# Eight FFN rounds behind an attention stage: low parts on VectorE, longer route leads, conversions split around the token chunks

## The chip, the cores and the metric

The kernel runs on one core of one Trainium2 chip. The metric is the device time of one execution in microseconds (us), as the median of runs; lower is better. Engines are named as in the profile: PE is the matmul engine (PEld its weight load), DVE is VectorE, ACT is ScalarE, POOL is GpSimd, SP issues most of the DMAs.

## The reference

Three stages in float32. First an mLSTM-like attention over 4 batches, 8 heads, 768 steps and head size 40 gives x with 3072 rows of 320. Then a mixture of experts, in which each token goes to one of 8 experts of 384 places, handed out in falling order of all logits:

```python
logits = x @ w_gate
for idx in np.argsort(-logits.flatten()):
    tok, e = idx // 8, idx % 8
    if assigned[tok] >= 0 or counts[e] >= 384: continue
    assigned[tok] = e; counts[e] += 1
for e in range(8):
    mask = assigned == e
    y[mask] = np.maximum(x[mask] @ w1[e], 0.0) @ w2[e]   # 320 -> 1024 -> 320
```

Last a gated layer that is the same for all tokens: `out = ((y @ w_a) * (y @ w_b)) @ w_out`, 320 to 1536 to 320.

## The kernel before, in words

The attention stage (up to about 200 us) is not touched. Behind it come eight **rounds**, one for each expert in the order in which experts fill up (`ffn`, L1000). A round takes its 384 tokens through both layers:

- *g phase*: `g1(f)` (L1040, 8 matmuls each, f = 0 to 7) makes a 128x384 piece of the hidden layer from the token tiles xh, xl and the expert's weights w1h, w1l; `g2(f)` (L1051, 8 matmuls each) adds it into three sums called acc with w2.
- *handover* (L1082 to L1090): the three sums become yh and yl.
- *ab phase*: `ab(f)` (L1095, 16 matmuls, f = 0 to 11) makes a and b, and `outp(f)` (L1113, 9 matmuls of 320 columns) adds the product into the output sums. `tail` (L1136) writes a round's output rows, within the next round.

Every float32 factor is split into a **high part** (an ACT copy to float32r) and a **low part** (the value minus the high part), so each product needs up to three matmuls. Low parts of the hidden pieces are tiles `ml`: in the g phase DVE makes them (L1048) right behind the ACT high part, in the ab phase POOL does (L1110), once for each f. The next expert's weights are loaded raw and converted by `split_w` (L907), eight pieces a round: for w1 ACT makes w1h (L914), POOL the low part w1l (L918), DVE the low part of the last 64 rows (L919); for w2 ACT makes the high part (L926), POOL two low parts (L927 of 2x64, L929 of 2x256 columns).

Which tokens come next is found by `route(r)` (L667), a chain that runs beside the matmuls of the round before: DVE compares keys with 128 thresholds (three tiles `G` for one count, L660), PE counts with 24 small matmuls (`rt`, L684), DVE tests the count (`okb`, L703), PE sums that over the rows (L706), DVE makes new thresholds (`d`, L712), five times over; then an L752 step, and `place` (L789), which ends in the token list `idx` and PE's L817. `keys` (L618) begins the next route at once. Only DVE and PE work on it, and each is in order, so a late `G` stops PE in the middle of the round's matmuls.

The order is written out while the program is built: `mm` (L981) counts 0.155 for each matmul, and the generators (route, next weights, late conversions) go on when the count reaches what they last yielded. The numbers after `yield` thus say how many matmuls PE gets between two steps; they are leads, not waits. Route yields are multiplied by 1.25 from route 2 on. The next weights (`weights`, L845) start at the handover: load, wait for idx, gather the tokens by an indirect DMA on POOL (`xg`, L857), convert all eight pieces, then transpose the tokens (`prep_x`, L945, PE L955):

```python
        yield 1.0
        if r:
            yield from sw
...
        yield from self.prep_x(r, xg)
        yield from sw
```

In round 0 five late conversions of the shared layer's weights (`conv`, L115, with `rawb == 1`) run as well: DVE L121, L124, L127, ACT L133 and L135 (or L154), POOL L136 and L138 (or L155).

Of the kernel before, what the change touches and what calls it, by code (L numbers as in the profile page):

```python
# [43 lines left out]
class Kern:  # L44
# [70 lines left out]
    def conv(self, pool, kind, i, raw, more, nxt):  # L115
# [11 lines left out]
        V.tensor_tensor(F, F, sg, op=OP.mult)  # L127
# [539 lines left out]
    def route(self, r):  # L667
# [10 lines left out]
        def count(Gs, d, nthr):  # L678
# [14 lines left out]
            if r:  # L693
                yield 1.0
                for j in range(3):
                    mms(j)
# [3 lines left out]
        def total(cnt, on):  # L700
# [3 lines left out]
            yield 0.8  # L704
# [84 lines left out]
    def place(self, r, wm):  # L789
# [36 lines left out]
        if r:  # L826
            yield 1.0
            for j in range(3):
                mms(j)
# [15 lines left out]
    def weights(self, r):  # L845
# [4 lines left out]
        if r == 0:  # L850
            for _ in range(2):
                next(sw)
        while r not in self.idx:
# [7 lines left out]
        if r:  # L861
            yield from sw
# [44 lines left out]
    def split_w(self, r):  # L907
# [3 lines left out]
        def one(j):  # L911
# [5 lines left out]
            e = V if r == 0 and j < 2 else P  # L917
            e.tensor_sub(l, raw[:, 0:2], h[:, 0:2].bitcast(F32))  # L918
# [4 lines left out]
        def two(i):  # L923
# [76 lines left out]
    def ffn(self):  # L1000
# [34 lines left out]
        for r in range(E):  # L1035
# [3 lines left out]

            def g1(f):  # L1040
# [7 lines left out]
                V.scalar_tensor_tensor(hl, p, 0.0, hh.bitcast(F32), op0=OP.max, op1=OP.subtract)  # L1048
                hq[f] = (hh, hl)

            def g2(f):  # L1051
# [3 lines left out]
                mm(yp[2], w[:, 256:384], hh, start=st, stop=False)  # L1055
                mm(yp[2], w[:, 256:384], hl, start=False, stop=sp)
                for m in range(2):
                    wh = w[:, m * 128:m * 128 + 128]
# [29 lines left out]
            for c in range(2):  # L1088
                self.split_act(yh, yl, c, yp[c])
# [5 lines left out]
            def ab(f):  # L1095
# [3 lines left out]
                for k in range(2):  # L1099
# [9 lines left out]
                e = V if r + 1 == E and f == NF2 - 1 else nc.gpsimd  # L1109
                e.tensor_sub(gl, gf, gh.bitcast(F32))  # L1110
# [118 lines left out]
```

## Time and profile before

| | us |
|---|---|
| median of 3 runs | 910.32 (910.04 to 911.11) |
| the profiled execution | 908.78 |
| its span, first to last instruction | 907.1 |
| PE busy in the span | 820.5 (90%) |
| DVE busy | 537.7 (59%) |
| POOL busy | 415.8 (46%) |
| ACT busy | 353.8 (39%) |
| mean granted clock | 0.957 of full |

The profiled execution is 1.7 us longer than its span and 1.5 us shorter than the median. Times below are us from the start of the span. The granted clock is PE's share of its full 2.4 GHz; it has two levels here, 1.0 and 0.5. Matmuls overlap, so their recorded lengths (some 340 ns) are about twice the step from one to the next.

### The profile page before, as it was taken

What the parts mean: (1) busy time and instruction counts of PE and PEld (TensorE: products, weight loads), DVE (VectorE), ACT (ScalarE), POOL (GpSimd) and SP (SyncE); (2) the same over time, 40 slices, a digit from 0 to 9 for tenths busy, and PEclk for the clock granted to TensorE, in tenths of its full rate; (3) what the DMA queues carried; (4) which work ended last, traced back from release to release, by engine and by line L of the source; (5) the groups of instructions that cost most, each with busy time, mean ns of one, the idle gap of its engine ahead of it and who ended that gap; (6) DMA issues with size and microseconds to landing.
All of it is one profiled execution on the core that took longest, in us unless ns stands there. A gap on an engine that the chain in (4) does not pass through costs nothing.

```text
span 907.1 us, 15899 instructions
## 1 busy us (share of the span) xinstructions
PE 820.5 (90%) x5939; PEld 777.9 (86%) x5939; DVE 537.7 (59%) x1188; ACT 353.8 (39%) x721; POOL 415.8 (46%) x440
## 2 busy tenths in 40 slices
PE   5779889885888899979989999999999999999996
PEld 3678778774777889979879998999899999999996
DVE  6777888856866885676576587476764212311211
ACT  4877678610443332232233234224322532532321
POOL 4576777731423670464056338233723823532122
PEclk9998999995898989989989999999999999999999
DMA  6875777523222310220120122031111301200000
GB/s 180 256 222 168 232 231 216 151 69 85 66 66 83 93 51 16 75 76 19 57 74 24 35 81 59 1 96 48 30 53 45 106 24 44 76 1 23 1 1 22
DMA packets 51038, 73.84 MB, mean 81 GB/s; under 512 B 6161, under 2 KB 41361, under 8 KB 50961
## 3 DMA queue, kind: packets, MB, share of 16 engines
q1 hardware_dynamic: 41744, 45.30, 17.5%
q10 hardware_dynamic: 6912, 19.66, 6.6%
q0 software_dynamic: 2304, 7.87, 2.7%
q8 instruction: 47, 0.77, 0.4%
q14 instruction: 31, 0.25, 0.1%
HBM read 63.37 MB, written 7.86 MB: 79 GB/s over the span
## 4 chain that ended last, share of the span: by engine, by line
PE 66%; DVE 14%; ACT 10%; issue 4%; DMA 3%; POOL 1%; ACTq 1%; DVEq 0%; POOLq 0%; SPq 0%
PE ring L982 33%; PE acc L982 20%; DVE G L660 3%; PE pq L400 2%; PE rt L684 2%; PE pv L431 2%; DVE w1h L919 1%; ACT mq L194 1%; PE pe L392 1%; DVE gf L1105 1%; PE pl L490 1%; PE pg L416 1%; ACT dd L394 1%; DMA mraw<-in_wab_dram 1%; ACT yh L978 1%
## 5 line engine op out<-in xcount | busy, mean ns | idle before, releaser
L1110 POOL TENSOR_TENSOR ml<-gf,mh 128x384 fp32r<-128x384 f32 x95 | 106.6, 1122 | 266.4 <-ACT mh L1107 265.9
L982 PE MATMUL ring<-yh,wh 128*128 128x384 f32 x576 | 202.2, 351 | 6.4 <-ACT yh L978 4.6
L982 PE MATMUL ring<-yl,wh 128*128 128x384 f32 x576 | 136.8, 344 | 0.0
L982 PE MATMUL ring<-yh,wl 128*128 128x384 f32 x384 | 132.6, 345 | 0.0
L1105 DVE TENSOR_TENSOR gf<-ring,at 128x384 f32<-128x384 f32 x96 | 53.3, 555 | 127.2 <-PE ring L982 123.3
L1107 ACT ACTIVATE mh<-gf 128x384 fp32r<-128x384 f32 x96 | 50.4, 525 | 187.4 <-DVE gf L1105 187.4
L982 PEld LDWEIGHTS ring<-yh,wh 128*128 128x128 f32 x576 | 111.4, 193 | 13.8 <-ACT yh L978 7.2
L660 DVE TENSOR_TENSOR G<-thc,d 128x1024 bf16<-128x1024 int16 (+1 forms) x90 | 110.4, 1245 | 0.4
L982 PEld LDWEIGHTS ring<-yl,wh 128*128 128x128 f32 x576 | 105.6, 193 | 0.1
L982 PE MATMUL acc<-woh,ml 128*128 128x320 f32 x288 | 91.7, 318 | 0.0
L982 PE MATMUL acc<-woh,mh 128*128 128x320 f32 x288 | 90.7, 315 | 0.0
L982 PE MATMUL acc<-wol,mh 128*128 128x320 f32 x288 | 90.5, 314 | 0.0
L982 PE MATMUL acc<-mh,w 128*128 128x384 f32 x320 | 88.9, 341 | 0.0
L1046 ACT ACTIVATE mh<-ring 128x384 fp32r<-128x384 f32 x64 | 31.5, 492 | 133.3 <-PE ring L982 127.9
L1048 DVE SCALAR_TENSOR_TENSOR ml<-ring,mh 128x384 fp32r<-128x384 f32 x64 | 35.5, 556 | 79.4 <-ACT mh L1046 76.8
L1103 ACT ACTIVATE at<-ring 128x384 f32<-128x384 f32 x96 | 46.8, 487 | 79.9 <-PE ring L982 76.7
L982 PEld LDWEIGHTS ring<-yh,wl 128*128 128x128 f32 x384 | 74.3, 194 | 0.0
L918 POOL TENSOR_TENSOR w1l<-raw,w1h 128x512 fp32r<-128x512 f32 x30 | 43.9, 1468 | 51.2 <-ACT w1h L914 51.1
L982 PE MATMUL ring<-xh,w1h 128*128 128x384 f32 x192 | 65.9, 343 | 0.1
L982 PE MATMUL acc<-ml,w 128*128 128x384 f32 x192 | 65.2, 339 | 0.5 <-DVE ml L1048 0.5
L982 PEld LDWEIGHTS acc<-mh,w 128*128 128x128 f32 x320 | 58.6, 190 | 0.3 <-issue 0.3
L982 PEld LDWEIGHTS acc<-woh,ml 128*128 128x128 f32 x288 | 55.3, 192 | 2.5 <-POOL w L929 2.2
(212 smaller groups left out, 1721.6 us busy)
## 6 DMA issues: line engine op xcount, KB each, us to landing
raw<-in_moe_w_dram SPq DMA_DIRECT2D x32, 320.0 KB
raw<-in_moe_w_dram SPq DMA_DIRECT2D x32, 256.0 KB
vk<-in_vk_dram SPq DMA_DIRECT2D x24, 324.0 KB
qr<-in_qk_dram SPq DMA_DIRECT2D x48, 160.0 KB
mraw<-in_wab_dram ACTq DMA_DIRECT2D x12, 640.0 KB
raw<-in_moe_w_dram SPq DMA_DIRECT2D x64, 64.0 KB
og<-in_og_dram ACTq DMA_DIRECT2D x6, 640.0 KB
qr<-in_qk_dram SPq DMA_DIRECT2D x48, 80.0 KB
```

What stands on the lines that cost most here:

```text
L400: nc.tensor.matmul(pq[:, o:o + 2], qk[:, 4 + hp], qk[:, H + 2 * hp:H + 2 * hp + 2], start=True, stop=True)
L431: nc.tensor.matmul(pvf[:, 64 * h:64 * h + w], P[:, h], vkf[:, (DE + D) * h:(DE + D) * h + w], start=True, stop=True)
L660: self.nc.vector.tensor_tensor(G, self.thc[:, None, 0:nthr].to_broadcast(dims), d[:, i0:i0 + 8, None].to_broadcast(dims), op=op)
L684: nc.tensor.matmul(cnt[0:nthr], Gs[j][:, i], oh[:, 8 * j + i], start=(j + i == 0), stop=(j * 8 + i == NT - 1))
L918: e.tensor_sub(l, raw[:, 0:2], h[:, 0:2].bitcast(F32))
L982: self.nc.tensor.matmul(*a, **k)
L1046: A.activation(hh, p, AF.Relu)
L1048: V.scalar_tensor_tensor(hl, p, 0.0, hh.bitcast(F32), op0=OP.max, op1=OP.subtract)
L1103: A.activation(at, p[0], AF.Copy)
L1105: V.tensor_mul(gf, p[1], at)
L1107: A.activation(gh, gf, AF.Copy)
L1110: e.tensor_sub(gl, gf, gh.bitcast(F32))
```

## The change

- All low parts go to DVE: `ml` of the ab phase, w1l, and both w2 low parts. POOL keeps the indirect DMAs and, in the late conversions of round 0, gets one multiply (L127) from DVE.
- `ml` is no longer issued right behind its high part, but some matmuls later, within the `g2` or `outp` of an older piece (`late_low`, `lows`).
- Three route leads grow: 1.0 to 1.5 ahead of a count's and of `place`'s matmuls, 0.8 to 1.5 ahead of L706.
- The next weights wait a lead of 6.0 behind the load. About five of the eight pieces are converted ahead of `prep_x`, the others behind it, and these may run into the next round, where `g1(f)` asks for the pieces that it needs.
- The handover takes acc 0 first and acc 2 last (`g2` computes acc 2 last, too), and `ab(0)` orders its matmuls by what is ready.

```diff
@@ conv
-        V.tensor_tensor(F, F, sg, op=OP.mult)
+        (P if self.rawb == 1 else V).tensor_tensor(F, F, sg, op=OP.mult)
@@ route.count, place
-                yield 1.0
+                yield 1.5
@@ route.total
-            yield 0.8
+            yield 1.5
@@ weights
+        else:
+            yield 6.0
...
         if r:
-            yield from sw
+            for c in (5.0, 3.0):
+                while c > 0:
+                    d = next(sw, None) or 0.6
+                    c -= d
+                    yield d
@@ split_w
-            e = V if r == 0 and j < 2 else P
-            e.tensor_sub(l, raw[:, 0:2], h[:, 0:2].bitcast(F32))
+            V.tensor_sub(l, raw[:, 0:2], h[:, 0:2].bitcast(F32))
...
-            P.tensor_sub(self.w2[:, 2 * i:2 * i + 2, DM:DM + 64], raw[:, :, 256:320],
+            V.tensor_sub(self.w2[:, 2 * i:2 * i + 2, DM:DM + 64], raw[:, :, 256:320],
                          h[:, :, 256:320].bitcast(F32))
-            P.tensor_sub(self.w2[:, 2 * i:2 * i + 2, DM + 64:], raw[:, :, 0:256], h[:, :, 0:256].bitcast(F32))
+            yield 1.0
+            V.tensor_sub(self.w2[:, 2 * i:2 * i + 2, DM + 64:], raw[:, :, 0:256], h[:, :, 0:256].bitcast(F32))
             self.more_raw()
-            yield 2.4
+            yield 1.4
...
-            w = sum(f)
+            yield from f
             self.wdone = k + 1
-            yield w
@@ ffn, g1 and g2
-                V.scalar_tensor_tensor(hl, p, 0.0, hh.bitcast(F32), op0=OP.max, op1=OP.subtract)
+                late_low.append(lambda: V.scalar_tensor_tensor(hl, p, 0.0, hh.bitcast(F32), op0=OP.max,
+                                                               op1=OP.subtract))
...
                 for m in range(2):
+                    if m:
+                        lows()
...
-                while r == 0 and self.wdone < (1, 3, 5, 7)[f // 2] + 1:
+                while self.wdone < ((1, 3, 5, 7)[f // 2] + 1 if r == 0 else f // 2 + (4 if f >= 2 else 1)):
                     next(ws[1])
@@ ffn, handover
+            self.split_act(yh, yl, 0, yp[0])
+            A.activation(yh[:, 1], yp[1], AF.Copy)
             A.activation(yb, yp[2][64:128], AF.Copy)
             V.tensor_add(ys, yp[2][0:64], yb)
-            for c in range(2):
-                self.split_act(yh, yl, c, yp[c])
+            V.tensor_sub(yl[:, 1], yp[1], yh[:, 1].bitcast(F32))
             self.split_act(yh, yl, 2, ys)
@@ ffn, ab and outp
-                e = V if r + 1 == E and f == NF2 - 1 else nc.gpsimd
-                e.tensor_sub(gl, gf, gh.bitcast(F32))
+                late_low.append(lambda: V.tensor_sub(gl, gf, gh.bitcast(F32)))
...
                 for t in rows:
+                    if t == 1:
+                        lows()
...
-                for _ in ws[1]:
-                    pass
+                while r + 1 not in self.xh:
+                    next(ws[1], None)
```

The line numbers of the changed program are some 5 to 30 higher (L660 stays; L918 is now L923, L919 L924, L927 L932, L929 L935, L982 L987, L1105 L1135, L1110 L1139).

DVE near the end of round 1, where the first count of the next route is made (d are the thresholds, oh the one-hot experts, G what PE's count reads). Before:

```order
L644 SCALAR_TENSOR_TENSOR d_4613<-d_4617,pen 128x24
L919 TENSOR_TENSOR w1h<-raw,w1h 64x256
L646 TENSOR_TENSOR oh<-w_241,code 128x192
L660 TENSOR_TENSOR G<-thc,d_4613 128x1024
L1105 TENSOR_TENSOR gf<-ring,at 128x384
L660 TENSOR_TENSOR G<-thc,d_4613 128x1024
L919 TENSOR_TENSOR w1h<-raw,w1h 64x256
L660 TENSOR_TENSOR G<-thc,d_4613 128x1024
```

and now:

```order
L644 SCALAR_TENSOR_TENSOR d_4727<-d_4731,pen 128x24
L1135 TENSOR_TENSOR gf<-ring,at 128x384
L1139 TENSOR_TENSOR ml<-gf,mh 128x384
L646 TENSOR_TENSOR oh<-w_241,code 128x192
L660 TENSOR_TENSOR G<-thc,d_4727 128x1024
L923 TENSOR_TENSOR w1l<-raw,w1h 128x512
L924 TENSOR_TENSOR w1h<-raw,w1h 64x256
L660 TENSOR_TENSOR G<-thc,d_4727 128x1024
L923 TENSOR_TENSOR w1l<-raw,w1h 128x512
L924 TENSOR_TENSOR w1h<-raw,w1h 64x256
L1135 TENSOR_TENSOR gf<-ring,at 128x384
L660 TENSOR_TENSOR G<-thc,d_4727 128x1024
```

The three G of the count now have the w1 low parts and an `ml` between them, in DVE's own queue.

PE at the handover of round 6 (acc are the sums of the g phase, ring the first tiles of the ab phase). Before:

```order
L982 MATMUL acc<-mh,w_2485 128x384 x2
L982 MATMUL acc<-ml,w_2485 128x384
L982 MATMUL ring<-yh,wh_69 128x384
L982 MATMUL ring<-yh,wl_70 128x384
L982 MATMUL ring<-yh,wh_69 128x384
L982 MATMUL ring<-yh,wl_70 128x384
L982 MATMUL ring<-yh,wh_69 128x384
L982 MATMUL ring<-yl,wh_69 128x384 x3
```

and now:

```order
L987 MATMUL acc<-mh,w_2485 128x384
L987 MATMUL acc<-ml,w_2485 128x384
L987 MATMUL ring<-yh,wh_69 128x384
L987 MATMUL ring<-yh,wl_70 128x384
L987 MATMUL ring<-yh,wh_69 128x384
L987 MATMUL ring<-yh,wl_70 128x384
L987 MATMUL ring<-yh,wh_69 128x384
L987 MATMUL ring<-yh,wl_70 128x384
L987 MATMUL ring<-yh,wh_69 128x384
L987 MATMUL ring<-yh,wl_70 128x384
L987 MATMUL ring<-yl,wh_69 128x384 x4
L987 MATMUL ring<-yh,wh_69 128x384 x2
L987 MATMUL ring<-yl,wh_69 128x384 x2
```

What needs the third part of yh, which is ready last, moved from the fifth matmul to the thirteenth.

POOL in round 0, from the first to the second late conversion (mu is the value under work, msg its sign). Before:

```order
L136 TENSOR_TENSOR wl_2471<-mu,wh_2470 128x512
L138 TENSOR_TENSOR mtl<-mu,mth 128x128
L155 TENSOR_TENSOR wol_2477<-mu,woh_2476 128x640
L1110 TENSOR_TENSOR ml<-gf,mh 128x384 x3
L136 TENSOR_TENSOR wl_2473<-mu,wh_2472 128x512
```

and now:

```order
L127 TENSOR_TENSOR mu<-mu,msg 128x640
L136 TENSOR_TENSOR wl_2471<-mu,wh_2470 128x512
L138 TENSOR_TENSOR mtl<-mu,mth 128x128
L127 TENSOR_TENSOR mu<-mu,msg 128x640
L155 TENSOR_TENSOR wol_2477<-mu,woh_2476 128x640
L127 TENSOR_TENSOR mu<-mu,msg 128x640
L136 TENSOR_TENSOR wl_2473<-mu,wh_2472 128x512
```

POOL's `ml` are gone from between the conversions, and the multiply stands ahead of each.

## Rows read from the trace of the kernel before

**Rows 1.** Rounds 0, 1, 6: length; busy PE, PEld, DVE, ACT, POOL; PEclk, DMA share, GB/s

```profile
229.70:333.70 104.00, 88.76 (x630) 83.91 (x628) 80.75 (x154) 40.15 (x74) 53.57 (x45) 0.89 0.24 73
333.70:422.60 88.90, 82.97 (x616) 78.84 (x616) 58.85 (x125) 27.62 (x54) 35.22 (x35) 0.96 0.15 45
...
751.50:825.20 73.70, 73.31 (x440) 72.34 (x439) 17.42 (x32) 26.48 (x51) 30.64 (x33) 1.00 0.12 37
```

**Rows 2.** What PE waited for, 303 to 676 us: total, times, longest

```profile
PE rt L684 <- DVE G L660: 12.8, 7, 4.2
PE rt L706 <- DVE okb L703: 4.8, 4, 2.1
```

**Rows 3.** PE's timeline, waits in rounds 3 and 4: start, us, [idle before]

```profile
547.87 0.16 PE L706 MATMUL rt<-ok,on 128*128 128x1 bf16 x1 [1.95 <-DVE okb L703]
...
638.61 0.35 PE L684 MATMUL rt<-oh,G 128*128 128x8 bf16 x8 [1.04 <-DVE G L660]
```

**Rows 4.** Stretches around the waits that end at 319, 548, 639, columns as in rows 1

```profile
316.90:323.70 6.80, 4.69 (x23) 4.38 (x24) 5.14 (x14) 2.11 (x4) 4.90 (x5) 0.50 0.35 96
549.00:552.40 3.40, 3.40 (x13) 3.40 (x12) 3.34 (x3) 1.44 (x3) 3.40 (x3) 0.51 0.25 81
638.00:645.00 7.00, 6.39 (x45) 6.24 (x46) 6.53 (x13) 3.81 (x7) 6.88 (x7) 1.00 0.23 70
```

**Rows 5.** DVE's timeline ahead of the wait at 319

```profile
307.17 4.08 DVE L644 SCALAR_TENSOR_TENSOR d<-d,pen 128x24 int16<-128x24 int32 x1
311.17 0.35 DVE L646 TENSOR_TENSOR oh<-w,code 128x192 bf16<-128x192 f32 x1
...
316.78 2.18 DVE L660 TENSOR_TENSOR G<-thc,d 128x1024 bf16<-128x1024 int16 x1
```

**Rows 6.** POOL's timeline beside it

```profile
307.70 1.30 POOL L918 TENSOR_TENSOR w1l<-raw,w1h 128x512 fp32r<-128x512 f32 x1
...
316.43 3.66 POOL L918 TENSOR_TENSOR w1l<-raw,w1h 128x512 fp32r<-128x512 f32 x2
```

**Rows 7.** DVE's groups by shape, rounds 1 to 4: busy us, mean ns

```profile
L660 DVE TENSOR_TENSOR G<-thc,d 128x1024 bf16<-128x1024 int16 x54 | 76.2, 1427 | 0.1
...
L660 DVE TENSOR_TENSOR G<-thc,rr 128x1024 bf16<-128x1024 int16 x15 | 18.2, 1218 | 0.1
...
L919 DVE TENSOR_TENSOR w1h<-raw,w1h 64x256 fp32r<-64x256 f32 x16 | 16.0, 1002 | 8.5 <-ACT w1h L914 6.9 <-ACT mh L1107 1.3
```

**Rows 8.** Single lines: ns min/median/max of low parts on DVE, POOL

```profile
L918 DVE TENSOR_TENSOR w1l<-raw,w1h x2: 692/694/695, 221.4 to 223.1; 128x512 fp32r<-128x512 f32 x2
...
L1110 DVE TENSOR_TENSOR ml<-gf,mh x1: 558/558/558, 896.6 to 896.6; 128x384 fp32r<-128x384 f32 x1
...
L919 DVE TENSOR_TENSOR w1h<-raw,w1h x30: 422/605/4491, 233.4 to 786.7; 64x256 fp32r<-64x256 f32 x30
...
L155 POOL TENSOR_TENSOR wol<-mu,woh x2: 1563/2052/2542, 266.8 to 300.3; 128x640 fp32r<-128x640 f32 x2
```

**Rows 9.** The chain that ended last, 478 to 486 us: start, us, what

```profile
480.10 2.80 PE ring L982 x16
```

**Rows 10.** Timelines at the handover of round 6

```profile
776.77 0.44 PE L982 MATMUL ring<-yh,wh 128*128 128x384 f32 x1 [0.33 <-ACT yh L978]
...
774.23 0.49 ACT L1085 ACTIVATE yb<-acc 64x384 f32<-64x384 f32 x1 [2.63 <-PE acc L982]
...
775.66 1.06 ACT L978 ACTIVATE yh<-ys 64x384 fp32r<-64x384 f32 x2
```

**Rows 11.** What PE waited for, 229.7 to 303 us (round 0)

```profile
PE rt L684 <- DVE G L660: 4.4, 4, 2.4
PE rt L752 <- DVE ok L749: 2.5, 1, 2.5
PE ring L982 <- ACT yh L978: 2.1, 1, 2.1
PE ring L982 <- ACT yh L974: 1.4, 1, 1.4
```

More of the change, by code (lines that the diff above doesn't have):

```diff
@@ L826, in place @@
         if r:
-            yield 1.0
+            yield 1.5
             for j in range(3):
@@ L1038, in ffn, with lows @@
             yp = None
+            late_low = []
+            def lows():
+                while late_low:
+                    late_low.pop(0)()
             def g1(f):
@@ L1062, in g2 @@
                     mm(yp[m], wh, hl, start=False, stop=sp)
+                mm(yp[2], w[:, 256:384], hh, start=st, stop=False)
+                mm(yp[2], w[:, 256:384], hl, start=False, stop=sp)
             for f in range(NF1):
-                while r == 0 and self.wdone < (1, 3, 5, 7)[f // 2] + 1:
+                while self.wdone < ((1, 3, 5, 7)[f // 2] + 1 if r == 0 else f // 2 + (4 if f >= 2 else 1)):
                     next(ws[1])
@@ L1074, in ffn @@
                     g2(f - 2)
+                else:
+                    lows()
+            for _ in ws[1]:
+                pass
             g2(NF1 - 2)
+            lows()
             g2(NF1 - 1)
-            if r == 0:
-                for _ in ws[1]:
-                    pass
             if r + 1 < E:
+                self.wdone = 0
                 ws[:] = [self.now, self.weights(r + 1)]
@@ L1097, in ab @@
                 wh, wl = self.wh[f], self.wl[f]
-                for k in range(2):
+                if f == 0:
+                    for c in range(2):
+                        for k in range(2):
+                            mm(p[k], wh[:, 2 * k + c], yh[:, c], start=c == 0, stop=False)
+                            mm(p[k], wl[:, 2 * k + c], yh[:, c], start=False, stop=False)
+                    for c in range(2):
+                        for k in range(2):
+                            mm(p[k], wh[:, 2 * k + c], yl[:, c], start=False, stop=False)
+                    for k in range(2):
+                        mm(p[k], wh[:, 4 + k], yh[:, 2], start=False, stop=False)
+                    for k in range(2):
+                        mm(p[k], wh[:, 4 + k], yl[:, 2], start=False, stop=True)
+                for k in range(2 if f else 0):
                     self.proj(p[k], [wh[:, 2 * k + c] for c in range(2)], [wl[:, 2 * k + c] for c in range(2)],
@@ L1108, in ab @@
                 gl = fw.tile([128, CAP], F32R, name="ml", bufs=3)
-                e = V if r + 1 == E and f == NF2 - 1 else nc.gpsimd
-                e.tensor_sub(gl, gf, gh.bitcast(F32))
+                late_low.append(lambda: V.tensor_sub(gl, gf, gh.bitcast(F32)))
+                if f == NF2 - 1:
+                    lows()
                 gq[f] = (gh, gl)
@@ L1116, in outp @@
                 for t in rows:
+                    if t == 1:
+                        lows()
                     ts = slice(t * 128, t * 128 + 128)
@@ L1128, in ffn @@
                     outp(f - 2, op, gq)
+                else:
+                    lows()
             if r + 1 < E:
@@ L1132, in ffn @@
                     next(rs[1])
-                for _ in ws[1]:
-                    pass
+                while r + 1 not in self.xh:
+                    next(ws[1], None)
             def tail(r=r, op=op, gq=gq):
```

2 lines of the change are left out of this document (removed).

## The prediction

> **What bounds the kernel now.** I read the busy time by round first: a round with no route beside it (6) takes 73.7 us, with PE busy for 73.31 of them; round 1 takes 88.9 and round 0 takes 104.0 [rows 1]. Eight rounds like round 6 would be 590 us, and from 229.7 us to the end of the span there are 677. Some of the difference is route work on PE that stays whatever is done; the rest is PE standing still. The view of waits shows for what: from 303 us (late in round 0) to 676 PE waits 12.8 us for DVE's G and 4.8 us for its test okb, 17.6 us in all [rows 2]. The reader should see that the releaser is always DVE, in the middle of matmuls that have nothing to do with it.
>
> Second, what a wait costs afterwards. Around the longest (4.2 us, until 319) PE's granted clock is 0.50 (1.2 of 2.4 GHz) for 6.8 us; behind one of 1.95 us it is 0.51 for 3.4 us; around the two pieces before 639 (the second of 1.04) it stays 1.00 [rows 3, 4]. There are two more stretches of 6.8 us like the first, in rounds 1 and 2 (round 1's mean clock of 0.96 is one [rows 1]). So 3 x 6.8 + 3.4 = 23.8 us run at half clock, which costs half of that, 11.9 us.
>
> Third, why DVE is late. Its timeline before 319 shows an operation on 24 numbers (L644) that takes 4.08 us, until 311.25, and a G of 2.18 us [rows 5]; POOL's low parts of w1 start at 307.70 and fill that time and the time of that G (3.66 us from 316.43) [rows 6]. The same shape of G takes 1218 ns on average in `place`, where no conversion runs, but 1427 in the counts, and the w1h low part 1002 ns against 422 at the least [rows 7, 8]. In rounds 1 to 4 these two alone lose 54 x 0.209 + 16 x 0.58 = 20.6 us of DVE. So POOL stretches DVE, DVE stops PE, and PE's clock falls.
>
> The Trainium skill (SBUF — State Buffer, Who interferes with whom) says that a VectorE instruction with two SBUF inputs and a GpSimd one that reads SBUF exclude each other, and the later one blocks until the first ends. The trace agrees: the L644 above ends with POOL's third piece.
>
> **The change, part by part.** The sum is made against the profiled execution, 908.78 us, which is 1.54 us under the median of 910.32.
>
> *Low parts to DVE.* Each round adds 12 `ml` at 0.558, four w1l at 0.694, and four w2 pairs [rows 8]. The larger of a pair has 512 elements like w1l, so 0.694; for the small one (128 elements) I scale down from 558 ns at 384 and 694 at 512, which gives 0.286; bounds are 0 and the 0.422 of w1h's 256. Together 6.70 + 2.78 + 3.92 = 13.4 us a round. DVE is busy for 58.85 of 88.9 us in round 1 [rows 1], at least 5 of them stretched, so some 67 us of work meet a round of about 81 us: it fits, unless it comes at the wrong place.
>
> The wrong place is the end of a round, where the keys, the conversions and the first count meet. In the changed order 75 matmuls stand between `place`'s matmuls and the first count (71 before). A step of 384 columns costs 0.175 [rows 9], and all 428 of round 6 cost 0.172 on average (73.7 / 428); I take 0.17, so PE needs 75 x 0.17 = 12.7 us. DVE has to do in that time: three G (3.65), three w1l (2.08), three w1h (1.27), two gf and one `ml` (1.67), and sixteen operations on 192 numbers or fewer, 0.35 or less each [rows 5]; I put these at 0.2, 3.2 together: 11.9 us, behind another gf and `ml` (1.1). That is even, and an `ml` waits for ACT between. I expect PE to wait there still, 0 to 2 us, and take 1.0 in each of five rounds. Without the change the same sum is 9.3 us against 71 x 0.17 = 12.1, and PE yet waited: that is the stretching.
>
> *Longer leads.* A count's matmuls now come 48 matmuls behind L706 instead of 44 (+0.7 us), and L706 comes 18 behind the count instead of 12 (+1.0 us). They add no instruction. A route now spans 413 matmuls instead of 373, so idx of the next round stands at matmul 320 of 428 in round 1 and earlier in each later one; no round waits for it. If it came late, the end of the round would pay for all the rest of the route.
>
> *Late waits, first term.* 17.6 us become 5 x 1.0: **-12.6**. The 11.9 us of half clock go with them, less 1.1 us (a wait of 2.1 us lay inside such a stretch and lost nothing more there): **-10.8**. A wait of 1.04 left the clock alone [rows 3, 4], so I charge none for the rest.
>
> *Round 0.* Before 303 us PE waits 4.4 us for G, 2.5 us at L752, and 2.1 + 1.4 at the handover [rows 11]. The first count (3.2 of the 4.4) gains nothing: the low parts that POOL did beside DVE now stand in DVE's own queue; bounds -3.2 and +2. At the handover acc 0 and 1 are read first, so of 3.5 us some 0.5 stay: -3.0. The L752 wait stands behind a test on DVE; what made that late the row doesn't say, and I take half, -1.3. The mean clock of 0.89 means 2 x 0.11 x 104 = 22.9 us at half clock, of which 6.8 lie around 319 and some 16 earlier, for 8 us of cost [rows 1, 4]; with less than half of the waits gone I take 40% of it, -3.4. Together **-7.7**, bounds 0 and -18.
>
> *The multiply on POOL* (five, all in round 0): the nearest row is wol, also 640 columns, 1.56 to 2.54 us [rows 8]. DVE must not start the next conversion before POOL is done with mu, and a G can meet it. It costs PE between 0 and 5 x 2.5 = 12.7 us; POOL is otherwise idle now and the next conversion follows some 43 matmuls (7 us) later, so I take a low value, **+2**.
>
> By that rule of the Trainium skill (SBUF — State Buffer, Who interferes with whom) a multiply that meets a G would hold it to its own end; if all five did so, this term alone would be about +8 and the forecast 887.
>
> *Handovers of rounds 1 to 7.* PE now waits for the third part of yh. ACT first copies acc 1 (0.49 like yb), then come yb 0.49, the sum 0.56 and two ACT copies 1.06 [rows 8, 10]: 2.6 us, while twelve matmuls and the last step cover 13 x 0.175 = 2.3. So PE waits some 0.3 to 0.5 us, where it was 0.33: **0**, bounds -3 and +3 over seven rounds. Conversions that run into the next round lie beside its g phase; in the order each piece of w2 stands ahead of the `g2` that reads it by some 25 matmuls: 0. The lead of 6.0 behind the load lets ACT start on landed weights: 0. The indirect DMAs and `tail` are as before: 0.
>
> Sum: -12.6 - 10.8 - 7.7 + 2 = -29.1, so 879.7 for the profiled execution and with the 1.54 **881** for the median. This case's own bounds are 874 to 890.
>
> **The rivals.**
>
> *Everything drains (866).* DVE's instructions overlap (L646 starts 0.08 us before L644 ends [rows 5]), so its 13 us may be 10.5 and no wait is left: -5; the multiply hides: -2; round 0 gives 8 more of its bound. For it: clean durations fit. Against it: `ml` waits for ACT in DVE's queue.
>
> *Half the waits stay (898).* An `ml` or w1l that is not ready blocks the G behind it. If half of 17.6 us and half of the clock term stay, +3.8 and +5.4, and round 0 gives nothing, +7.7: 881 + 17.
>
> *VectorE becomes the bound (slower, 921).* From `place` to the second count of the next route the changed order gives DVE six G (7.3), four w1l and four w1h (4.5), three pieces of w2 (1.3), twelve gf, `ml` and xl (6.7) and 24 small operations (4.8): 24.6 us, against 141 matmuls, 24.0. If nothing overlaps and each of five `ml` waits 0.49 us for ACT, PE falls 3.1 us behind in each of the six rounds that now hold a route, and each such wait brings 3.4 us of lost clock: 6 x 6.5 = 39 instead of 28.4, and with nothing gained in round 0 that is 921. It decides from waits of some 1.9 us on, the least that the clock followed [rows 3, 4]. Against it: DVE is free for a third of round 1 even now.
>
> *No change (909).* If the waits are the chain's own latency and not POOL's doing, only the leads help; 13.4 us more on DVE take that back. The stretched G speak against it.
>
> **How the numbers follow.** Forecast 0.53, everything drains 0.17, half the waits stay 0.18, slower 0.08, no change 0.04. Faster by over 0.2% (about what a measurement of this kernel can tell from no change) are the first three: 0.88; same 0.04; slower 0.08. The range reaches from 866 to 904, which leaves out the last two and a little on either side.
>
> **What would show it.** In the new profile: G of the counts near 1220 ns and the w1h low part near 430; POOL nearly idle from round 1 on; DVE busy some 62 to 67 us in rounds 1 to 4; PE's waits for G and okb from round 1 on below 6 us; no half-clock stretch behind 303 us but perhaps one; rounds 1 to 4 at 80 to 82 us and round 0 at 92 to 97. Wrong it would be if G is short and PE waits all the same (then DVE's queue is the bound), if rounds 1 to 4 stay above 85 us, or if round 0 grows past 104.

## The result, and the profile after

The changed kernel takes 884.25 us (median, 882.35 to 887.58); the ratio to the kernel before is 0.9717 [0.9678, 0.9756], so 2.8% faster. The forecast was 881, with a range of 866 to 904. The profiled execution takes 882.35 (span 880.6) and stands 26.4 us below the 908.78 of before; the forecast for it was 879.7. Of the 26.4 us, 1.7 lie ahead of round 0, in the part that the change does not touch. Rounds 0 to 7 last 92.8, 81.7, 78.6, 81.5, 82.7, 80.8, 73.2 and 73.6 us.

The same view as [rows 1], rounds 0, 1 and 6 of the changed kernel (length; busy PE, PEld, DVE, ACT, POOL; PEclk, DMA share, GB/s):

```profile
227.95:320.78 92.83, 84.45 (x605) 80.63 (x605) 75.78 (x167) 38.59 (x72) 23.49 (x17) 0.94 0.26 78
320.78:402.43 81.65, 79.44 (x590) 75.81 (x589) 56.47 (x137) 27.20 (x54) 8.06 (x9) 1.00 0.17 48
...
726.11:799.26 73.15, 73.10 (x440) 72.36 (x439) 29.71 (x56) 26.57 (x51) 6.10 (x9) 1.00 0.14 41
```

In round 1 POOL falls from 35.2 to 8.1 us, and what is left there are indirect DMAs. DVE makes the low parts of all rounds and yet is busy for less time than before (56.5 against 58.9 us): its operations are no longer stretched, and one count of the route has moved out of the round. Round 0 loses 11.2 us and round 1 loses 7.3.

What PE waited for, 303 to 676 us, the view of [rows 2]:

```profile
PE rt L684 <- DVE G L660: 4.1, 5, 1.5
PE rt L706 <- DVE okb L703: 1.7, 3, 0.7
PE ring L987 <- DVE xl L984: 1.0, 1, 1.0
```

and 229 to 303 us, as in [rows 11]:

```profile
PE rt L706 <- DVE okb L703: 3.3, 2, 2.3
PE rt L752 <- DVE ok L749: 1.4, 1, 1.4
PE ring L987 <- DVE yl L980: 1.1, 1, 1.1
PE rt L684 <- DVE G L660: 1.0, 1, 1.0
PE ring L987 <- DVE yl L1107: 0.3, 1, 0.3
```

The late waits for G and okb fall from 17.6 to 5.8 us. The window ends at 676 us, where round 5 of the kernel before begins and its last route is over; in the changed kernel the last route runs on into round 5, and there PE waits another 2.1 us (0.62 and 1.50, for DVE's z, at L796). Early in round 0 the waits for G nearly go (4.4 to 1.0), but okb is new there (3.3).

DVE's groups by shape, rounds 1 to 4 (busy us, mean ns), against [rows 7]:

```profile
L660 DVE TENSOR_TENSOR G<-thc,d 128x1024 bf16<-128x1024 int16 x51 | 61.8, 1219 | 0.1
L1139 DVE TENSOR_TENSOR ml<-gf,mh 128x384 fp32r<-128x384 f32 x48 | 26.7, 557 | 23.0 <-ACT mh L1137 23.0
...
L935 DVE TENSOR_TENSOR w<-raw,w 128x512 fp32r<-128x512 f32 x20 | 13.6, 682 | 0.0
L923 DVE TENSOR_TENSOR w1l<-raw,w1h 128x512 fp32r<-128x512 f32 x16 | 11.0, 685 | 1.5 <-ACT w1h L920 1.5
L924 DVE TENSOR_TENSOR w1h<-raw,w1h 64x256 fp32r<-64x256 f32 x16 | 6.8, 423 | 0.5
L932 DVE TENSOR_TENSOR w<-raw,w 128x128 fp32r<-128x128 f32 x19 | 5.4, 284 | 1.4 <-ACT w L931 1.2
```

G takes 1219 ns instead of 1427 and the w1h low part 423 instead of 1002. On DVE's timeline near the end of round 0, where an operation on 24 numbers took 4.08 us [rows 5], the same one now takes 0.17:

```profile
307.14 0.17 DVE L644 SCALAR_TENSOR_TENSOR d<-d,pen 128x24 int16<-128x24 int32 x1
307.53 1.22 DVE L660 TENSOR_TENSOR G<-thc,d 128x1024 bf16<-128x1024 int16 x1
```

The longest late wait left is in round 4. PE's timeline, then DVE's:

```profile
626.53 0.36 PE L684 MATMUL rt<-oh,G 128*128 128x8 bf16 x8 [1.54 <-DVE G L660]
```

```profile
623.61 0.69 DVE L923 TENSOR_TENSOR w1l<-raw,w1h 128x512 fp32r<-128x512 f32 x1 [1.33 <-ACT w1h L920]
624.33 0.42 DVE L924 TENSOR_TENSOR w1h<-raw,w1h 64x256 fp32r<-64x256 f32 x1
624.78 0.56 DVE L1139 TENSOR_TENSOR ml<-gf,mh 128x384 fp32r<-128x384 f32 x1
625.26 1.22 DVE L660 TENSOR_TENSOR G<-thc,d 128x1024 bf16<-128x1024 int16 x1
```

A w1l stands at the head of DVE's queue and waits 1.33 us for ACT's copy; the G that PE needs stands three places behind it.

### The profile page after: what moved, and what is told of

Read it like the earlier page. It is cut to its first block, busy times and chain, and to the rows that moved or that the text cites. A ratio compares the mean times of both kernels' runs of the same rounds, so it can differ in the third digit from the quotient of the medians.

```text
span 880.6 us, 15866 instructions
## 1 busy us (share of the span) xinstructions
PE 808.4 (92%) x5939; PEld 768.9 (87%) x5939; DVE 576.9 (66%) x1372; ACT 354.0 (40%) x721; POOL 208.7 (24%) x256
## 4 chain that ended last, share of the span: by engine, by line
PE 58%; DVE 13%; issue 11%; ACT 8%; DMA 5%; POOL 3%; ACTq 0%; SPq 0%; DVEq 0%; POOLq 0%
PE ring L987 30%; PE acc L987 17%; PE rt L684 3%; PE pq L400 2%; DVE G L660 2%; PE pv L431 2%; DMA qr<-in_qk_dram 2%; DMA wh<-mth 2%; DVE gf L1135 1%; ACT mh L1137 1%; ACT mq L194 1%; PE pl L490 1%; PE pg L416 1%; DVE ml L1139 1%; PE pe L392 1%
## 5 line engine op out<-in xcount | busy, mean ns | idle before, releaser
L987 PE MATMUL ring<-yh,wh 128*128 128x384 f32 x576 | 196.6, 344 | 0.3 <-DVE xl L980 0.2
L987 PE MATMUL ring<-yl,wh 128*128 128x384 f32 x576 | 137.8, 342 | 1.6 <-DVE yl L980 1.1
L987 PE MATMUL ring<-yh,wl 128*128 128x384 f32 x384 | 130.9, 341 | 0.0
L987 PEld LDWEIGHTS ring<-yh,wh 128*128 128x128 f32 x576 | 108.6, 190 | 6.5 <-issue 3.3
L987 PEld LDWEIGHTS ring<-yl,wh 128*128 128x128 f32 x576 | 104.0, 191 | 5.5 <-DVE yl L1107 2.6
L1135 DVE TENSOR_TENSOR gf<-ring,at 128x384 f32<-128x384 f32 x96 | 53.3, 555 | 73.5 <-PE ring L987 62.6
L660 DVE TENSOR_TENSOR G<-thc,d 128x1024 bf16<-128x1024 int16 (+1 forms) x90 | 95.6, 1075 | 0.4
L1184 POOL DMA_INDIRECT out_dram<-ot,idx x24 | 27.1, 1131 | 287.1 <-ACT ot L1182 280.3
L987 PE MATMUL acc<-woh,mh 128*128 128x320 f32 x288 | 90.2, 313 | 0.0
L987 PE MATMUL acc<-woh,ml 128*128 128x320 f32 x288 | 89.9, 312 | 0.0
L987 PE MATMUL acc<-wol,mh 128*128 128x320 f32 x288 | 89.8, 312 | 0.0
L859 POOL DMA_INDIRECT xg<-xd,idx x24 | 24.9, 1037 | 265.9 <-PE ring L987 136.8
L987 PE MATMUL acc<-mh,w 128*128 128x384 f32 x320 | 86.6, 335 | 0.0
L1139 DVE TENSOR_TENSOR ml<-gf,mh 128x384 fp32r<-128x384 f32 x96 | 54.0, 563 | 47.2 <-ACT mh L1137 47.0
L987 PEld LDWEIGHTS ring<-yh,wl 128*128 128x128 f32 x384 | 72.7, 189 | 1.8 <-issue 1.8
L987 PE MATMUL ring<-xh,w1h 128*128 128x384 f32 x192 | 66.3, 345 | 0.0
L987 PE MATMUL acc<-ml,w 128*128 128x384 f32 x192 | 64.5, 336 | 0.0
L987 PEld LDWEIGHTS acc<-mh,w 128*128 128x128 f32 x320 | 58.2, 188 | 0.0
```

The costliest lines, as they stand in the source:

```text
L660: self.nc.vector.tensor_tensor(G, self.thc[:, None, 0:nthr].to_broadcast(dims), d[:, i0:i0 + 8, None].to_broadcast(dims), op=op)
L859: self.nc.gpsimd.indirect_dma_start(out=xg[:, t], out_offset=None, in_=self.xd, in_offset=bass.IndirectOffsetOnAxis(ap=self.idx[r][:, t:t ...
L987: self.nc.tensor.matmul(*a, **k)
L1135: V.tensor_mul(gf, p[1], at)
L1139: late_low.append(lambda: V.tensor_sub(gl, gf, gh.bitcast(F32)))
L1184: st = nc.gpsimd.indirect_dma_start(out=self.out, out_offset=bass.IndirectOffsetOnAxis(ap=self.idx[r][:, t:t + 1], axis=0), in_=ot[:, t], ...
```

## The experiments

A ratio is to the kernel before, with its 95% interval; the kernel before was timed again in each group. One per cent of it is 9.1 us. The expectations in front of each run speak of the median.

| run | edit | us | ratio |
|---|---|---|---|
| the change | | 884.25 | 0.9717 [0.9678, 0.9756] |
| 1 | changed kernel, low parts back on POOL | 901.93 | 0.9909 [0.9862, 0.9957] |
| 2 | kernel before, low parts on DVE in their old places | 906.84 | 0.9956 [0.9920, 0.9992] |
| 3 | changed kernel and unused work on POOL | 911.91 | 1.0013 [0.9969, 1.0057] |
| 4 | changed kernel, old leads | 891.23 | 0.9785 [0.9743, 0.9826] |
| 5 | kernel before, longer leads | 910.80 | 0.9996 [0.9969, 1.0023] |
| 6 | changed kernel, split undone | 898.98 | 0.9845 [0.9823, 0.9867] |
| 7 | changed kernel, old leads and split undone | 893.11 | 0.9831 [0.9800, 0.9861] |
| 8 | changed kernel, `ml` at once | 886.70 | 0.9728 [0.9697, 0.9760] |
| 9 | changed kernel, old handover | 889.41 | 0.9758 [0.9725, 0.9791] |
| 10 | changed kernel, multiply on DVE | 879.64 | 0.9689 [0.9654, 0.9723] |
| 11 | changed kernel, lead between w1h and its low parts | 877.86 | 0.9656 [0.9629, 0.9683] |
| 12 | 10 and 11 together | 875.00 | 0.9620 [0.9578, 0.9663] |

**Whose doing: POOL's work beside DVE, or DVE's queue?** Runs 1 to 3.

Run 1:

```diff
-            V.tensor_sub(l, raw[:, 0:2], ...)
+            (V if r == 0 and j < 2 else P).tensor_sub(l, raw[:, 0:2], ...)
...
-            V.tensor_sub(self.w2[...DM:DM + 64], ...); V.tensor_sub(self.w2[...DM + 64:], ...)
+            P.tensor_sub(self.w2[...DM:DM + 64], ...); P.tensor_sub(self.w2[...DM + 64:], ...)
...
-                late_low.append(lambda: V.tensor_sub(gl, ...))
+                late_low.append(lambda: (V if r + 1 == E and f == NF2 - 1 else P).tensor_sub(gl, ...))
```

> The changed kernel with all low parts (w1l, both of w2, ml of the ab phase) back on POOL, at the places and with the leads of the changed kernel. If POOL stretching DVE is what made PE wait: the counts' G go back to some 1400 ns and w1h to some 1000, PE's waits for G and okb from round 1 on rise from about 6 us to 12 or more, some half-clock stretches come back, and the time is 892 to 905. If the longer leads did it: G may stretch, but the leads cover it, and the time stays at 882 to 888. If what counts is only how much work DVE has: less of it, and the time falls below 882.

The move itself is worth 1.9% (0.9909 against 0.9717). In rounds 1 to 4 of this run:

```profile
L660 DVE TENSOR_TENSOR G<-thc,d 128x1024 bf16<-128x1024 int16 x51 | 74.4, 1474 | 0.2
...
L924 DVE TENSOR_TENSOR w1h<-raw,w1h 64x256 fp32r<-64x256 f32 x16 | 9.5, 593 | 4.0 <-ACT w1h L920 3.7
```

G is as long as before, and PE waits for it for 12.8 us from 303 to 676 again. The w1h low part is stretched less than expected (593 ns, not some 1000), and the time falls in the range given for stretching.

Run 2 does nothing but the move: the four operations of the kernel before go from POOL to DVE, in the same places.

```diff
-            e = V if r == 0 and j < 2 else P
-            e.tensor_sub(l, raw[:, 0:2], ...)
+            V.tensor_sub(l, raw[:, 0:2], ...)
...
-            P.tensor_sub(self.w2[...
+            V.tensor_sub(self.w2[...
...
-                e.tensor_sub(gl, ...)
+                V.tensor_sub(gl, ...)
```

> The kernel before with its low parts on DVE, each where POOL had it, and nothing else. If POOL's stretching was the cause: G near 1220 ns, w1h near 430, half or more of the gain alone, 885 to 898, although DVE has 13 us more a round. If the leads and the new order were the cause: DVE's queue is longer and nothing covers it, 905 to 925.

The contention theory alone missed here. One DVE group and PE's waits, 303 to 676 us:

```profile
L660 DVE TENSOR_TENSOR G<-thc,d 128x1024 bf16<-128x1024 int16 x54 | 65.2, 1218 | 0.1
```

```profile
PE rt L684 <- DVE G L660: 9.4, 5, 3.6
PE rt L706 <- DVE okb L703: 7.4, 8, 1.5
```

G is short and the stretching is gone, yet PE waits 16.8 us (17.6 before). DVE's timeline ahead of the longest of these waits, 3.57 us until 471.09, for the third G of a count:

```profile
467.02 0.69 DVE L917 TENSOR_TENSOR w1l<-raw,w1h 128x512 fp32r<-128x512 f32 x1
467.74 0.42 DVE L918 TENSOR_TENSOR w1h<-raw,w1h 64x256 fp32r<-64x256 f32 x1
...
469.34 0.56 DVE L1108 TENSOR_TENSOR ml<-gf,mh 128x384 fp32r<-128x384 f32 x1 [0.59 <-ACT mh L1106]
469.82 1.22 DVE L660 TENSOR_TENSOR G<-thc,d 128x1024 bf16<-128x1024 int16 x1
```

The low parts now stand in DVE's queue ahead of G: what no longer stretches it now precedes it. So the move gains 0.4% in the old order and 1.9% in the new one.

Run 3 leaves all low parts on DVE and gives POOL eight subtractions a round into a tile `g` that nothing reads, one for each piece converted:

```diff
             V.tensor_sub(l, raw[:, 0:2], h[:, 0:2].bitcast(F32))
+            if r:
+                P.tensor_sub(g, h[:, 0:2].bitcast(F32), h[:, 0:2].bitcast(F32))
...
+            if r:
+                P.tensor_sub(g, h[:, :, 0:256].bitcast(F32), h[:, :, 0:256].bitcast(F32))
```

> The changed kernel plus eight subtractions a round on POOL from round 1's conversions on: of 512 columns, of the new high parts from themselves, into a tile that nobody reads, so nothing waits for them and no result changes. If two SBUF readers on DVE and POOL exclude each other: the counts' G rise to 1300 ns or more and w1h to 600 or more, PE's waits from round 1 on rise by 4 us or more, 888 to 900. If POOL's part in it was that somebody waited for its results, or its place in the order: 883 to 886, as without them.

It costs more than the range of the exclusion theory: 3.0%, some 27 us, and the whole gain is gone. DVE's groups in its rounds 1 to 4, then POOL's:

```profile
L660 DVE TENSOR_TENSOR G<-thc,d 128x1024 bf16<-128x1024 int16 x51 | 67.0, 1322 | 0.2
L660 DVE TENSOR_TENSOR G<-thc,rr 128x1024 bf16<-128x1024 int16 x12 | 14.6, 1220 | 0.1
L923 DVE TENSOR_TENSOR w1l<-raw,w1h 128x512 fp32r<-128x512 f32 x16 | 12.6, 788 | 1.5 <-ACT w1h L920 1.5
```

```profile
L941 POOL TENSOR_TENSOR thr<-w 128x512 f32<-128x512 f32 x19 | 27.4, 1441 | 56.6 <-ACT w L934 56.2
L926 POOL TENSOR_TENSOR thr<-w1h 128x512 f32<-128x512 f32 x16 | 19.3, 1208 | 27.2 <-ACT w1h L920 26.5
```

POOL is busy for 46.7 us in four rounds with work that no one waits for, and the G that meet it grow, while those of `place`, beside which it does nothing, stay at 1220. G grows by 8% only; what stands ahead of it in DVE's queue grows more: the w1h low part from 423 to 558 ns (expected were 600), `ml` from 557 to 645, the larger w2 low part from 682 to 869. That work on POOL alone stretches DVE is shown by this run, for it adds nothing to DVE's or PE's queue; whether POOL's reads or its writes do it, no run separates.

**Leads and split.** Runs 4 to 7. Run 4 puts the three yields back:

```diff
-                yield 1.5
+                yield 1.0
...
-            yield 1.5
+            yield 0.8
```

> The changed kernel with the three route leads back at 1.0, 0.8 and 1.0. If POOL's stretching was the cause, the short leads cost little now: 0.7 us per count and 1.0 us per test are missing only where DVE is late, so 885 to 893 with G still near 1220 ns. If the leads were the cause: 898 or more.

Run 5 does the reverse in the kernel before.

> The kernel before with the three longer route leads and nothing else. Theory A (leads and the move work on different causes, the chain's latency and the stretching of DVE): what the leads give in the changed kernel (7 us) they give here too: 902 to 905, with G still near 1430 ns and the w1h low part near 1000. Rival B (with POOL's low parts stretching DVE the leads cannot cover the waits, since these are longer than a lead): 907 to 912. Rival C (leads are all that the whole change needs): below 895.

Run 4 takes 891 us, inside the range given for stretching, with G at 1218 ns. In the changed kernel the leads are worth 0.7% (the two intervals just overlap), in the kernel before nothing (rival B); G even grows there, to 1593 ns. PE's waits of run 5, 303 to 676 us, show why:

```profile
PE rt L684 <- DVE G L660: 11.4, 8, 3.0
PE ring L982 <- ACT xh L974: 2.1, 2, 1.1
...
PE rt L706 <- DVE okb L703: 0.6, 1, 0.6
```

The wait for okb went (4.8 to 0.6) and that for G hardly did, but the next round now waits for its tokens xh. The split is what that calls for. Run 6 undoes it alone:

```diff
-            for c in (5.0, 3.0):
-                while c > 0:
-                    d = next(sw, None) or 0.6
-                    c -= d
-                    yield d
+            yield from sw
```

> The changed kernel, but all eight pieces are converted ahead of the token chunks, as before; the lead of 6.0, the late low parts and the rest stay. Theory A (DVE's queue): the conversions of all eight pieces then meet the keys and the first count of the next route, and the token chunks come last, at the end of the round; the waits at the ends of rounds 0 to 4 grow by 0.5 to 1.5 us each, the median from 884 to 888 to 895. Rival B (the split only moves work that lies beside PE anyway): 884, within 2 us.

It costs 1.3%, some 12 us and more than theory A said, and in another place: not conversions and keys at a round's end, but the next round's start. PE at the start of its round 1, then ACT just before:

```profile
325.39 1.15 PE L956 MATMUL ring<-identf,xg 128*128 128x128 f32 x9
330.38 0.69 PE L983 MATMUL ring<-xh,w1h 128*128 128x384 f32 x1 [3.84 <-ACT xh L975]
```

```profile
329.21 0.74 ACT L927 ACTIVATE w<-raw 128x640 fp32r<-128x640 f32 x1 [2.62 <-DMA raw<-in_moe_w_dram]
329.85 0.85 ACT L975 ACTIVATE xh<-ring 128x384 fp32r<-128x384 f32 x2
```

The transposes are done at 326.5. ACT's copy xh stands behind the last w2 copy in ACT's queue, and that one waits 2.62 us for raw weights to land. In all, PE waits 7.1 us for xh and xl from 303 to 676 us (1.2 in the changed kernel), and behind the starts of rounds 1 to 3 it runs at half clock for a while (a mean of 0.54 from 329 to 336 us). With the split, xh goes ahead of the last pieces, and these may be late.

Run 7 undoes both.

> The changed kernel with both undone: the three leads at their old values and all eight pieces converted ahead of the token chunks. Leads undone alone gave 891, the split undone alone 899. Theory A (they are a pair: longer leads make a route later, and only then do eight conversions ahead of the token chunks make the next round's xh late): 889 to 894, no wait for xh, and L684 and L706 as with the leads undone alone. Rival B (the split is worth 15 us by itself, since conversions crowd the end of the round whatever the route's length): 902 to 909, with xh waits.

The median is in theory A's interval, and no wait for xh is in its trace. By the ratios, undoing the split costs 0.5% with the old leads (0.9785 to 0.9831, with intervals that overlap) and 1.3% with the longer ones (0.9717 to 0.9845, clear of each other); the longer leads gain 0.7% with the split and nothing without it. They are a pair.

**The smaller parts.** Run 8 issues each `ml` right behind its high part.

```diff
+            def at_once(f):
+                f()
...
-                late_low.append(lambda: V.scalar_tensor_tensor(hl, ...))
+                at_once(lambda: V.scalar_tensor_tensor(hl, ...))
...
-                late_low.append(lambda: V.tensor_sub(gl, ...))
+                at_once(lambda: V.tensor_sub(gl, ...))
```

> The changed kernel, but each low part of a hidden piece (ml, g and ab phase) is issued right behind its high part on ACT, as in the kernel before, and not some matmuls later. Theory A (DVE's queue is what the move had to be paid in): an ml that stands in DVE's queue before ACT has made its high part holds every G, okb and d behind it by up to 0.5 us, 20 times a round; PE's waits for G and okb behind 303 us grow from 5.8 to 10 to 16 us and the median from 884 to 889 to 898. Rival B (the low parts' place is of no account, because DVE is free for a third of the time): 884, within 2 us, and the same waits.

The difference of 0.1% is inside both intervals, and the late waits are 7.5 instead of 5.8 us. Theory A fell: where an `ml` stands hardly matters. The later place does not even spare DVE the wait for ACT: in the changed kernel the 48 `ml` of the ab phases in rounds 1 to 4 still wait 23.0 us for it (the row of L1139 above), 0.48 each.

Run 9 puts back the handover, the order in `g2` and that of `ab(0)`:

```diff
-            self.split_act(yh, yl, 0, yp[0])
-            A.activation(yh[:, 1], yp[1], AF.Copy)
...
-            V.tensor_sub(yl[:, 1], yp[1], yh[:, 1].bitcast(F32))
+            for c in range(2):
+                self.split_act(yh, yl, c, yp[c])
             self.split_act(yh, yl, 2, ys)
...
-            for k in range(2 if f else 0):
+            for k in range(2):
```

> The changed kernel with the handover, the order within g2 and the order of ab(0) put back as before. Theory A (the handover gives 0.5 us in each round, as the lengths of rounds 6 and 7 show: 73.15 against 73.65): about 4 us in eight rounds, the median from 884 to 887 to 890, rounds 6 and 7 at 73.6 with a wait of 0.3 us for yh each, and round 0 up by 1 to 3. Rival B (my forecast: the new order waits for the third part of yh as long as the old one for the first): 884, within 1 us.

Rounds 6 and 7 last 73.66 and 74.13 again, and each of rounds 1 to 7 is 0.5 to 0.6 us longer than in the changed kernel, 3.7 together. Round 0 did not grow but fell by 1.1 (to 91.75): that part of the expectation missed. The ratio says 0.4%, with intervals that overlap.

Run 10 puts the multiply L127 back on DVE.

```diff
-        (P if self.rawb == 1 else V).tensor_tensor(F, F, sg, op=OP.mult)
+        V.tensor_tensor(F, F, sg, op=OP.mult)
```

> The changed kernel with the multiply of the late conversions (L127, five in round 0) back on DVE. Theory A (on POOL it holds the small operations of the route, which stand 1.4 to 1.5 us instead of 0.17 to 0.35, and so makes PE's waits for okb of 2.3 and 1.0 us and for L752 of 1.4 us): these waits go or fall below 0.5, round 0 falls from 92.8 to 88 to 90, the median to 879 to 882. Rival B (five multiplies of 640 columns, some 0.8 us each, take their time in DVE's queue instead): round 0 at 92 to 95, the median at 884 to 887.

Round 0 falls to 90.2 us, but not for the reason expected. In the changed kernel DVE and POOL stood so:

```profile
268.16 1.52 DVE L736 SCALAR_TENSOR_TENSOR tb<-k,lo 128x24 int32<-128x24 int32 x1
```

```profile
268.10 1.53 POOL L127 TENSOR_TENSOR mu<-mu,msg 128x640 f32<-128x640 f32 x1 [5.10 <-DVE k L734]
```

With the multiply on DVE (0.82 us), L736 takes 0.18. Yet PE waits longer for okb, 5.8 us before 303 instead of 3.3. For the longest of these waits (3.01 us until 265.54) DVE's own multiply is not the reason, for it starts at 265.40, behind okb. Counted from the start of round 0, this okb starts 1.6 us sooner than in the changed kernel, but PE is there 2.3 us sooner. What is shorter is the time at half clock: round 0's mean clock is 0.97 there against 0.94. And of the 5.1 us between the profiled executions (882.35 and 877.21) 2.65 lie ahead of round 0, where the two programs are the same. Since the intervals of run 10 and of the change overlap as well, whether the multiply on POOL costs anything stays unclear.

Run 11 puts a lead between ACT's copy and the low parts that read it, for all pieces of w1:

```diff
             A.activation(h, raw, AF.Copy)
-            if r == 0 and j < 2:
-                yield 1.0
+            yield 1.0
             V.tensor_sub(l, raw[:, 0:2], h[:, 0:2].bitcast(F32))
...
-            yield 2.4
+            yield 2.4 if r == 0 and j < 2 else 1.4
```

> The changed kernel with a lead of 1.0 between ACT's copy w1h and the low parts of w1 on DVE in all pieces (and 1.0 less behind them). Theory A (what is left of the waits comes from a w1l at the head of DVE's queue that waits for ACT, 1.33 us ahead of the wait of 1.54 at 626.75): the waits for G behind 303 us fall from 4.1 to 1 to 2.5 us, the half-clock stretch in round 4 goes, the median falls by 2 to 5 us to 879 to 882. Rival B (DVE's queue is simply full there, and a low part that waits costs no more than one that runs later): 883 to 886 and the waits as they are.

It gains another 0.6%: the intervals of run 11 and of the change just overlap, and from the start of round 0 to the end its profiled execution is 7.0 us shorter. In round 4 DVE has ACT's copy before it gets there, and this w1l now stands behind the G that PE needs:

```profile
622.37 0.56 DVE L1138 TENSOR_TENSOR ml<-gf,mh 128x384 fp32r<-128x384 f32 x1 [0.59 <-ACT mh L1136]
622.85 1.22 DVE L660 TENSOR_TENSOR G<-thc,d 128x1024 bf16<-128x1024 int16 x1
623.98 0.68 DVE L922 TENSOR_TENSOR w1l<-raw,w1h 128x512 fp32r<-128x512 f32 x1
```

and PE's waits, 303 to 676 us, are

```profile
PE rt L706 <- DVE okb L703: 3.3, 4, 2.0
PE rt L684 <- DVE G L660: 0.8, 2, 0.6
```

G's waits go (4.1 to 0.8), part of them turns into waits for okb (1.7 to 3.3), and no half-clock stretch is left in rounds 1 to 5 (the last section says why that is in part luck). Whether the shorter wait for ACT or the place behind G does it, this run does not separate.

Run 12 has the edits of 10 and 11.

> The changed kernel with both: the lead of 1.0 between w1h and the low parts of w1, and the multiply L127 back on DVE. Theory A (the two gains are of different places: the lead takes the waits of rounds 1 to 5 and gave 6 us, the multiply shortens round 0 by 2 to 4 us): 872 to 876, round 0 at 88 to 91, rounds 1 to 5 as with the lead alone (79.2 to 81.1). Rival B (in round 0 both act on the same wait, the okb of the second count, so the multiply adds nothing): 876 to 880, round 0 at 90 to 92.

875.0, ratio 0.9620, the lowest of all, though its interval overlaps run 11's. Rounds 1 to 4 are as in run 11. Round 0 lasts 90.0 against 91.0 there, so the multiply gives 1.0 us and not the 2 to 4 of theory A, and round 5 lasts 80.9 instead of 79.4. From the start of round 0 to the end the profiled executions last 646.2 (run 12) and 645.7 us (run 11): that the multiply adds anything to run 11 is not shown.

## Why the prediction was right, and where not

**Late waits.** Forecast 17.6 to 5.0, measured 5.8: right, in size and mostly in place. Of the 4.1 us for G 3.6 are at the first counts, where the sum of 11.9 us of DVE against 12.7 of PE was even; they come as 1.2, 0.4, 0.4 and 1.5 us, and as none at the end of round 2. The 2.1 us in round 5, behind this window, were not foreseen.

**Their cause, "the stretching".** Half right. The chain "POOL stretches DVE, DVE stops PE" is shown by run 3. But the prediction priced the move as if the order would come with it for nothing; run 2 shows that with the stretching gone and the order kept, DVE's queue makes nearly the same waits (16.8 us, and 0.4% instead of 2.8%). The rule of the Trainium skill (SBUF — State Buffer, Who interferes with whom) that was named there agrees with run 3, where the w1h low part takes 558 ns instead of 423. It says what stretches, not what is gained by a move. Of the 2.4% between run 2 and the change, leads and split are worth 1.1% (run 7 against the change).

**The leads and the split.** They were given no price of their own: leads "add no instruction", and "no round waits" for idx. That holds for the changed kernel, but only because of the split: without it xh is up to 3.84 us late (run 6). The prediction looked at where idx stands; what was late was ACT's queue behind the weights' DMA. Once, at 323.44, the changed kernel waits 1.0 us for xl, too.

**DVE's load.** Forecast 62 to 67 us in rounds 1 to 4; round 1 shows 56.5. The added work was sized well: `ml` 557 ns, w1l 685, the w2 pair 682 and 284 (taken as 558, 694, 694 and 286). The mis-sized term is "at least 5" us of stretching a round: 58.9 and 13.4 added make 72.3, one count of three G and its small operations moved out of the round (about 4), and 56.5 are left, so about 12 us a round were stretched. The rival in which VectorE becomes the bound does not rest on it but on a sum of clean lengths (24.6 us of DVE against 24.0 of PE). That `ml` waits for ACT, as this rival says, is so (0.48 us each); but PE did not fall 3.1 us behind in each of six rounds: its late waits for G and okb are 5.8 us in all.

**Clock.** Forecast -10.8 for the late stretches. In the kernel before 23.8 us ran at half clock there; in the changed one it is one stretch in round 4, behind the wait of 1.54. Two stretches from the end of that wait (columns as in [rows 1]):

```profile
626.75:630.15 3.40, 3.40 (x22) 3.31 (x19) 2.68 (x10) 1.57 (x3) 0.00 (x0) 0.72 0.43 125
630.15:633.00 2.85, 2.85 (x16) 2.66 (x15) 0.90 (x5) 0.85 (x2) 0.00 (x0) 0.74 0.11 38
```

A mean of 0.72 and 0.74 over 3.4 and 2.85 us is 2 x (0.28 x 3.4 + 0.26 x 2.85) = 3.4 us at half clock, which cost 1.7. So 11.9 became 1.7: -10.2, right in size. The rule behind it was not: the bound of "some 1.9 us" does not hold. In the kernel before, the stretch in round 2 (clock 0.50 from 470.5 to 477.3) already began behind waits of 1.35 and 0.78 us, when one of 1.82 had only started; in the changed kernel 1.54 was followed by a stretch, and in run 11 a wait of 1.96 by none (see the last section). That just one stretch is left is thus partly luck.

**Round 0.** The forecast of -7.7 is for the time before 303 us alone. With +2 for the multiply and what the late terms hold of round 0 (the wait of 4.2 until 319 down to 1.0, and half of its 6.8 us at half clock) it is -12.3 for the whole round; measured were -11.2. That is near, but its parts cancel. The first count, "gains nothing", lost its whole wait of 3.2 us, and POOL's low parts are the reason: with them back on POOL (run 1) PE waits there 0.99 and 2.26 us again, and with the bare move (run 2) 1.82. The handover kept 1.4 us of waits instead of 0.5. And okb waits 3.3 us where it waited for nothing, beside the multiply. L752 gave 1.1 of the 1.3 forecast. By the mean clock 2 x 0.06 x 92.83 = 11.1 us still run at half clock, against 22.9. (The clock term there has a slip: 40% of 8 is 3.2, not 3.4.)

**Handovers of rounds 1 to 7.** Forecast 0, measured -0.5 us each (rounds 6 and 7 of run 9): a mis-sized term of some -3.5 us. PE's wait of 0.33 on yh is gone, and no other came: the twelve matmuls cover what ACT does.

**Rounds.** 1 to 4 were forecast at 80 to 82 and came at 78.6 to 82.7, two of them inside; round 0 was forecast at 92 to 97 and came at 92.8. Round 5 grew by 5.8 us, because longer leads push the end of the last route into it (with the old leads, runs 4 and 7, it lasts 74.8); against that, rounds 0 to 2 each hold one count less.

**The sum.** -29.1 was forecast and -26.4 measured between the profiled executions. The sum is closer than its terms: 1.7 of the 26.4 lie ahead of round 0, which no term covers, and the handovers gave some 3.5 that were put at nothing; against these stand the longer round 5 and okb in round 0. That the total came out so near is partly luck.

**Open.** From run 2 (0.9956) to run 7 (0.9831) lies 1.3%, which the late `ml` (0.1%), the handover (0.4%) and the multiply (of the other sign) do not fill. The lead of 6.0 behind the load and the conversions issued piece by piece are candidates for the rest; no run tried them alone.

## What to carry to other kernels

Before moving work off an engine that disturbs another, ask what stands in the second engine's queue just ahead of the thing that is waited for: taking away the disturbance and keeping the order gave 0.4%, with leads and a new order 2.8%. An instruction whose input is made by another engine a moment earlier should be issued with a lead behind that; four such leads a round were worth another 0.6%. A longer lead makes what hangs on the end of the chain later, and it pays only if that can come before work that may be late.

## What the runs showed that was not expected

The clock does not follow the length of a wait alone. Runs 11 and 12 have the same program from round 1 on, and their rounds 1 to 4 agree within 0.05 us. At the end of round 4 PE waits for the same okb, in run 11 and then in run 12:

```profile
642.52 0.16 PE L706 MATMUL rt<-ok,on 128*128 128x1 bf16 x1 [1.96 <-DVE okb L703]
```

```profile
639.99 0.16 PE L706 MATMUL rt<-ok,on 128*128 128x1 bf16 x1 [1.95 <-DVE okb L703]
```

and behind it, in the same order (columns as in [rows 1]):

```profile
642.70:646.10 3.40, 3.40 (x22) 3.40 (x23) 2.82 (x6) 0.93 (x3) 0.27 (x1) 1.00 0.02 5
```

```profile
640.20:643.60 3.40, 3.40 (x14) 3.40 (x14) 1.95 (x4) 0.27 (x1) 0.00 (x0) 0.56 0.02 5
```

After the same wait, with the same matmuls ahead of it and the clock at 1.00, PE ran at 2.4 GHz in run 11 and mostly at 1.2 in run 12. That accounts for the longer round 5 of run 12 (80.9 against 79.4 us). Longer waits show the same in one place of round 0: behind 2.33 us in the changed kernel the mean clock is 0.53 (270.0 to 273.4), behind 3.01 us in run 10 it is 1.00 (265.6 to 269.0), behind 3.03 us in run 12 no half clock follows either, and behind 3.58 us in run 11 it is 0.65 (272.4 to 275.8). What decides besides the wait stays open here. A single profiled execution with or without such a stretch thus says little about an edit worth 1 or 2 us.

The second thing is how far a little work on POOL reaches: 46.7 us of it in four rounds, some 12 a round, cost 27 us of the kernel's time, though G grew by 8% only (1219 to 1322). From 303 to 676 us PE waits for G 18.5 us in run 3 against 4.1, and for okb 4.7 against 1.7, 17.4 more together. The rest is the clock: in the same stretch of time some 27 us run at half clock against 3.4, which costs about 12.
